# Decoding the output weights of a gated unit in three phases, and four moves of work in a fused attention, expert and gated-unit kernel

## The chip, the cores and the metric

The kernel runs on one core of a Trainium2 chip. The metric is the device time of one execution in microseconds. Five engines work side by side, each through its own queue in order: PE (TensorE, matrix products; its weight loads are shown apart as PEld), DVE (VectorE), ACT (ScalarE), POOL (GpSimd) and SP (SyncE, which issues most transfers).

## The reference

```
x   = attention(q, k, v, s)            # 4 x 8 heads, 576 rows of 64, causal, with a bias of cumulated s
e   = argmax(x @ w_gate); p = softmax's weight of e         # one expert of 8 for each of 2304 rows
x   = p * (relu(x @ w1[e]) @ w2[e])                         # 512 -> 1024 -> 512
xn  = x / sqrt(mean(x*x) + 1e-6) * rms_g
g   = xn @ moe2_w_gate;  val = xn @ moe2_w_val              # 512 -> 1536
out = (g * sigmoid(g) * val) @ moe2_w_out                   # 1536 -> 512
```
The three weights of the gated unit come as 64-bit floats. Products are made in single precision from a high and a low half of each operand, in three passes (high by high, high by low, low by high).

## The kernel before

**Stages.** Attention and routing come first, then the expert products (`moe`), then the gated unit (`glu`). PE, DVE and ACT run in the order in which the code issues (a manual schedule; for SP in `moe` too); POOL's order is set by the scheduler of the tile framework.

**Expert products.** `moe` runs eight slots. Slot 0 takes the first 256 rows of expert 0. For each of eight column blocks f, `gemm1` (L767) makes a hidden block; ACT writes its relu h in high halves (L770) and DVE the low halves (L771). `gemm2` (L783) makes four column blocks y from all eight f. Its first block needs the h of f = 0, 1, 2 ... one after another. Between the `gemm1` blocks of slot 0, `rank(n)` runs the next n steps of the last routing generator, small DVE instructions (L426 to L537) that place the rows and order the experts; the table `RANK` says how many steps before f = 0 and after each f.

After slot 0 come 128 more rows of expert 0 (`xl`, called the fill expert's rows here) in another form: their gate is applied by ACT (L722), `turn_tile` (L749 to L752) transposes them, `rows_gemm1` (L821, L823) makes the hidden rows `hr`, `turn_tile` transposes these into `hb`, with the low half by DVE (L752), and `rows_gemm2` (L832) multiplies. Its result is normed by `scaled_rows` (L839 to L842), called the yr chain here. The x of slot 1 is transposed beside it by `x_transpose` (L738 to L742). `finish` norms a slot's y: a product with ones (L805), a square root by ACT (L807), a reciprocal and four products by DVE (L808, L811); `keep` sends y to memory through SP. `split` makes high and low halves of the next expert weights (ACT L650, POOL L651).

**Gated unit.** `glu_head` is a generator that slot 7 of `moe` advances by one step after each f and each column block; it loads and decodes the first gated weights and splits the first rows `gx` (`glu_split_x`, L1038, L1039). `decode` turns two loads of 64-bit floats (`raw`) into single precision: on DVE two shifts of the low word (L1004), two joins with the high word (L1006); on ACT an absolute value (L1008); on DVE a maximum (L1010), a shift (L1012), an or (L1014) and the copy of the high half (L1016); on POOL the low half (L1017). There are four `raw` buffers.

The first product (L1061) goes over 12 blocks f, each for six groups g of 384 rows. The second product goes over `k.seq`, 72 steps: first f = 0 to 11 with g = 0 and 1 in turn (24 steps), then the other groups. A step (L1086) is nine matmuls, three passes for three tiles t of 128 rows. Its hidden block is split six steps ahead by ACT (L1076) and POOL (L1077) into a ring of twelve. Output weights 6 to 11 are decoded during the first 12 steps, two loads in each step with g = 1. After a group's last f ACT copies the three results (L1089) and POOL scatters them (L1090):

```
        if n < 24 and g == 1 and f + 6 < NF:
            decode(k, weights[0:2])
            weights = weights[2:]
            if f + 8 < NF:
                weights += load_out(k, f + 8)
        if n + ahead < len(k.seq):
            glu_split(k, n + ahead)
        glu_gemm2(k, acc, n)
```

Of the kernel before, what the change touches and what calls it, by code (L numbers as in the profile page):

```python
# [7 lines left out]
F32 = mybir.dt.float32  # L8
# [848 lines left out]
def moe(k, close):  # L857
# [40 lines left out]
    y = finish(k, 0, NA)  # L898
# [3 lines left out]
    turn_tile(k, k.hr[:, 512:1024], *[t[:, 4:8] for t in hb])  # L902
    split(k)
    x_transpose(k, 1, (2, 3), first)
    row = ids(k, k.x[1], first)
    keep(k, y, NA, 0)
    yr = y_tile(k, "yr")[:, 0:1024].rearrange("p (a n) -> p a n", a=2)
    k.yr = yr[:, 0, :]
    rows_gemm2(k, hb)
    keep_ids(k, row, column(k, 2))  # L910
# [44 lines left out]
RANK = (9, 0, 17, 10, 0, 0, 0, 0, 0)  # L955
# [43 lines left out]

def decode(k, loads):  # L1000
    nc = k.nc
    both = [(raw[:, :, 0], raw[:, :, 1], raw.bitcast(F32)[:, :, 1], w) for raw, w in loads]
    for low, high, hf, w in both:
        nc.vector.tensor_scalar(low, low, 29, None, op0=ALU.logical_shift_right)  # L1004
    for low, high, hf, w in both:
        nc.vector.scalar_tensor_tensor(low, high, 0xC0000000, low, op0=ALU.bitwise_and, op1=ALU.bitwise_or)  # L1006
    for low, high, hf, w in both:
        nc.scalar.activation(hf, hf, AF.Abs)  # L1008
    for low, high, hf, w in both:
        nc.vector.tensor_scalar(hf, hf, TINY, None, op0=ALU.max)  # L1010
    for low, high, hf, w in both:
        nc.vector.tensor_scalar(high, high, 3, 0x3FFFFFFF, op0=ALU.logical_shift_left, op1=ALU.bitwise_and)  # L1012
    for low, high, hf, w in both:
        nc.vector.tensor_tensor(high, high, low, op=ALU.bitwise_or)  # L1014
    for low, high, hf, w in both:
        nc.vector.tensor_copy(w[:, 0, :], hf)  # L1016
        nc.gpsimd.tensor_tensor(w[:, 1, :], hf, w[:, 0, :].bitcast(F32), op=ALU.subtract)  # L1017
# [62 lines left out]
def glu_gemm2(k, acc, n):  # L1080
    g, f = k.seq[n]
    w, c = k.wo[f], k.ring[n % 12]
    for t in range(3):
        cols = slice(128 * t, 128 * t + 128)
        for i, (a, b) in enumerate(((0, 0), (0, 1), (1, 0))):
            k.nc.tensor.matmul(acc[g][t], c[:, a, cols], w[:, b, :], start=f == 0 and i == 0, stop=f == 11 and i == 2)  # L1086
        if f == 11:
            o = new_raw(k).bitcast(F32).rearrange("p d two -> p (d two)")
            k.nc.scalar.copy(o, acc[g][t])  # L1089
            i = k.nc.gpsimd.indirect_dma_start(  # L1090
                out=k.out, out_offset=bass.IndirectOffsetOnAxis(ap=k.oid[:, g, t:t + 1], axis=0),
                in_=o, in_offset=None, bounds_check=NTOK - 1, oob_is_err=False,
            )
            of_rows(k, k.outs, i.ins, ())


def glu_head(k):
    glu_first(k)
    for g in range(3):
        glu_load(k, g)  # L1100
        if g == 0:
            weights = load_weights(k, 0)
    yield
    yield
    decode(k, weights[0:2])
    yield
    decode(k, weights[2:4])
    yield
    for n in (0, 0, 0, 0, 1, 2, 3, 4):
        if n:  # L1110
            glu_split_x(k, (n - 1) // 2, slice(2 * ((n - 1) % 2), 2 * ((n - 1) % 2) + 2))
        if n in (2, 4):
            glu_load(k, 2 + n // 2)
        yield


def glu(k):
# [66 lines left out]
    ahead = 6  # L1184
    for n, (g, f) in enumerate(k.seq):
        if f == 0:
            acc[g] = [k.psum.tile([128, 512], F32, name=f"go{k.uid()}", tag="b") for _ in range(3)]
        if n < 24 and g == 1 and f + 6 < NF:
            decode(k, weights[0:2])
            weights = weights[2:]  # L1190
            if f + 8 < NF:
                weights += load_out(k, f + 8)
        if n + ahead < len(k.seq):
            glu_split(k, n + ahead)
        glu_gemm2(k, acc, n)
# [185 lines left out]
```

## Time and profile before

| | |
|---|---|
| median of three runs | 929.44 us (929.34 to 929.82) |
| the profiled execution | 934.07 us, span 932.3 us |
| mean granted clock of TensorE | 0.988 of full speed |
| PE busy | 889.3 us, 95% of the span, 5684 matmuls |
| DVE, ACT, POOL busy | 460.2, 410.8, 332.9 us (49%, 44%, 36%) |
| attention and routing | to about 210 us of the span |
| expert products | about 210 to 460 us |
| first, second product of the gated unit | 460 to 761, 761 to 922 us |

Times in the profile are counted from the start of the span. A wait is an engine's idle time in front of an instruction, put down to what released it. Busy shares are averages over stages with different limits; what a stage is worth is read in the stage.

### The profile page before, as it was taken

Reading aid. Unit: us, or ns where it says so; the run is one execution under the profiler, and the core shown is the slowest. Engines: PE = TensorE matmul, PEld = TensorE weight load, DVE = VectorE, ACT = ScalarE, POOL = GpSimd, SP = SyncE. Lnnn points to the kernel's source line nnn. Section 1 sums busy time; section 2 is a strip of 40 time slices with the busy share of each in tenths; the row PEclk is TensorE's granted clock in tenths of the full one; section 3 lists DMA queues with packets and bytes.
Section 4 is the critical chain, followed back from the end, with each engine's and each line's share of the span. In section 5 each row is a group of like instructions: output and inputs, shape, how many; then the busy total and the mean of one; then the engine's idle time right before and its main releaser. Section 6 shows DMA issues by size and latency. Waiting matters only on the chain.

```text
span 932.3 us, 15830 instructions
## 1 busy us (share of the span) xinstructions
PE 889.3 (95%) x5684; PEld 781.1 (84%) x5684; DVE 460.2 (49%) x1339; ACT 410.8 (44%) x1009; POOL 332.9 (36%) x320
## 2 busy tenths in 40 slices
PE   6999999998799999999899999999999998899995
PEld 3666666668699999999899999999999995588884
DVE  4555664637524354544685555444554699700000
ACT  5887887873655566665531111111111122333310
POOL 2001321034566667676111110011100146797541
PEclk9999999999999999999999999999999999999998
DMA  7996686323646566666531101111011122110001
GB/s 236 291 295 193 180 233 183 97 97 90 227 154 194 174 193 195 196 182 210 166 102 46 46 26 43 46 46 45 27 43 46 46 100 81 47 68 35 35 34 37
DMA packets 51388, 111.59 MB, mean 120 GB/s; under 512 B 6064, under 2 KB 14027, under 8 KB 51299
## 3 DMA queue, kind: packets, MB, share of 16 engines
q1 hardware_dynamic: 48339, 100.95, 35.7%
q0 software_dynamic: 2912, 9.46, 2.7%
q8 instruction: 47, 0.77, 0.3%
q14 instruction: 42, 0.34, 0.1%
q10 hardware_dynamic: 48, 0.07, 0.0%
HBM read 89.69 MB, written 20.76 MB: 118 GB/s over the span
## 4 chain that ended last, share of the span: by engine, by line
PE 84%; DVE 6%; issue 4%; POOL 3%; ACT 2%; DMA 1%; POOLq 0%; DVEq 0%; ACTq 0%
PE gg L1061 32%; PE g L783 11%; PE g L767 8%; PE go L1086 8%; PE t L306 6%; PE pvy L352 5%; PE s L261 5%; PE tl L380 3%; PE sm L274 2%; DVE raw L1014 1%; DVE raw L1004 1%; PE xp L738 1%; PE r L832 1%; POOL gx5b L1077 1%; PE r L821 1%
## 5 line engine op out<-in xcount | busy, mean ns | idle before, releaser
L1061 PE MATMUL gg<-gx,ws 128*128 128x384 f32 x1728 | 300.4, 335 | 0.0
L1061 PEld LDWEIGHTS gg<-gx,ws 128*128 128x128 f32 x1728 | 299.6, 188 | 0.1
L651 POOL TENSOR_TENSOR u<-raw,u 128x1024 fp32r<-128x1024 f32 x64 | 154.3, 2422 | 104.4 <-ACT u L650 100.4
L1017 POOL TENSOR_TENSOR ws<-raw,ws 128x256 fp32r<-128x256 f32 x48 | 36.7, 786 | 259.2 <-DVE ws L1016 259.2
L783 PE MATMUL g<-h,u 128*128 128x256 f32 (+7 forms) x768 | 109.0, 301 | 5.4 <-DVE h L771 4.2
L783 PEld LDWEIGHTS g<-h,u 128*128 128x128 f32 x768 | 104.5, 194 | 6.5 <-DVE h L771 4.6
L767 PE MATMUL g<-xt,u 128*128 128x256 f32 (+7 forms) x768 | 104.2, 295 | 0.0
L1067 ACT ACTIVATE gh<-gg 128x384 f32<-128x384 f32 x72 | 35.3, 491 | 152.9 <-PE gg L1061 152.9
L767 PEld LDWEIGHTS g<-xt,u 128*128 128x128 f32 x768 | 101.4, 188 | 0.8
L1008 ACT ACTIVATE raw<-raw 128x256 f32<-128x256 f32 x72 | 28.1, 442 | 124.9 <-DVE raw L1006 112.4
L287 ACT ACTIVATE p<-sc,nm 128x128 f32<-128x128 f32 (+3 forms) x128 | 72.4, 572 | 12.0 <-DVE nm L247 8.3
L1068 DVE TENSOR_TENSOR gh<-gg,gh 128x384 f32<-128x384 f32 x72 | 40.0, 555 | 74.8 <-ACT gh L1067 74.8
L247 DVE CUSTOM_DVE_ANT_0 sc<-s,in 128x128 f32<-128x128 f32 (+3 forms) x128 | 57.5, 489 | 39.0 <-PE s L264 19.9
L650 ACT CAST u<-raw 128x1024 fp32r<-128x1024 f32 x64 | 67.2, 1050 | 4.0 <-DMA raw<-in_w 4.0
L339 ACT COPY pt<-t 128x512 f32<-128x512 f32 (+3 forms) x160 | 62.2, 433 | 11.6 <-PE t L306 7.4
L306 PE MATMUL t<-ident,p 128*128 128x128 f32 x400 | 62.2, 281 | 1.6 <-ACT p L287 1.5
L1069 DVE TENSOR_TENSOR gh<-gg,gh 128x384 f32<-128x384 f32 x72 | 40.2, 558 | 44.8 <-PE gg L1061 41.6
L791 DVE TENSOR_TENSOR sq<-sq,sn 128x256 f32<-128x256 f32 (+7 forms) x24 | 15.7, 653 | 87.8 <-ACT sn L790 87.8
L352 PE MATMUL pvy<-pt,vp 128*64 128x512 f32 (+4 forms) x320 | 50.8, 433 | 1.5 <-ACT pt L339 0.8
L261 PE MATMUL s<-in 64*128 64x128 f32 (+3 forms) x256 | 51.5, 491 | 0.0
L306 PEld LDWEIGHTS t<-ident,p 128*128 128x128 f32 x400 | 43.8, 141 | 6.9 <-ACT p L287 2.2
L234 POOL COPY in<-in 64x64 f32<-64x64 f32 x32 | 8.0, 251 | 116.0 <-DMA in<-in_q 106.0
(232 smaller groups left out, 1207.4 us busy)
## 6 DMA issues: line engine op xcount, KB each, us to landing
raw<-in_w SPq DMA_DIRECT2D x64, 512.0 KB, 4.3
in<-cumd SPq DMA_DIRECT2D x30, 256.0 KB, 5.1
xs<-zrow SPq DMA_DIRECT2D x8, 771.0 KB, 10.2
raw<-in_wg SPq DMA_DIRECT2D x24, 256.0 KB
raw<-in_wv SPq DMA_DIRECT2D x24, 256.0 KB, 3.0
raw<-in_wo SPq DMA_DIRECT2D x24, 256.0 KB, 2.6
vp<-in_v SPq DMA_DIRECT2D x16, 320.0 KB, 5.9
in<-in_q SPq DMA_DIRECT2D x16, 288.0 KB, 5.3
```

The source lines that it names most:

```text
L247: k.nc.vector.tensor_tensor_reduce(out=out, in0=ps, in1=bias, scale=-0.125, scalar=3e38, op0=ALU.add, op1=ALU.min, accum_out=accum)
L261: nc.tensor.matmul(ps[h], st.q[r, 128 * i:128 * i + 128], st.k[r, 0:w], start=True, stop=False)
L287: k.nc.scalar.activation(out, st.s[i, h][:, 0:w], AF.Exp, bias=st.nm[:, n:n + 1], scale=-1.0, accum_out=acc)
L306: nc.tensor.transpose(ps[:, off:off + 128], src[:, 128 * j:128 * j + 128], k.ident)
L339: nc.scalar.copy(b, a)
L352: nc.tensor.matmul(st.y[r, a - 64:512], st.v[:, h, j, :], k.pt[:, h, o:o + S - a], start=j == 0, stop=j == 4)
L650: nc.scalar.copy(w[:, :, 0, :], raw)
L651: nc.gpsimd.tensor_tensor(w[:, :, 1, :], raw, w[:, :, 0, :].bitcast(F32), op=ALU.subtract)
L767: nc.tensor.matmul(ps[:, 0:n], w[:, f % 4, a, 128 * kc:128 * kc + 128], x[b][:, kc, 0:n], start=kc == 0 and i == 0, stop=kc == 3 and i == 2)
L783: nc.tensor.matmul(ps[:, 0:n], w[:, f % 4, a, 128 * c:128 * c + 128], k.h[b][:, f, 0:n], start=f == 0 and i == 0, stop=f == 7 and i == 2)
L1061: nc.tensor.matmul(ps, w[:, m, a, 128 * kc:128 * kc + 128], b[:, kc, :], start=kc == 0 and n == 0, stop=kc == 3 and n == 2)
L1086: k.nc.tensor.matmul(acc[g][t], c[:, a, cols], w[:, b, :], start=f == 0 and i == 0, stop=f == 11 and i == 2)
```

## The change

It has five parts. (1) `finish` of slot 0 is issued after the transposes of `hb` and of slot 1's x instead of before them, its `keep` after `rows_gemm2`, and `yr` uses the buffer of `hr`. (2) `RANK` spreads the last ten steps of the ranking over the blocks after f = 2 to f = 7. (3) `glu_head` decodes in three phases, low, high and split, in successive steps, and its splits of `gx` come one step later. (4) In the second product the two loads of an output weight are decoded over three steps: low at g = 0, high at g = 1, split at the next g = 0, where ACT makes the copy of the high half; the split of the hidden block is issued ahead of them. (5) The last four steps of the last group go tile by tile instead of block by block, and the last result is copied in two halves by ACT and DVE.

```
@@ moe
-    y = finish(k, 0, NA)
     hb = [...]
     turn_tile(k, k.hr[:, 0:512], *[t[:, 0:4] for t in hb])
     x_transpose(k, 1, (0, 1), first)
     turn_tile(k, k.hr[:, 512:1024], *[t[:, 4:8] for t in hb])
+    x_transpose(k, 1, (2, 3), first)
     split(k)
-    x_transpose(k, 1, (2, 3), first)
+    y = finish(k, 0, NA)
     row = ids(k, k.x[1], first)
-    keep(k, y, NA, 0)
-    yr = y_tile(k, "yr")[:, 0:1024].rearrange("p (a n) -> p a n", a=2)
+    yr = k.hr.rearrange("p (a n) -> p a n", a=2)
     k.yr = yr[:, 0, :]
     rows_gemm2(k, hb)
+    keep(k, y, NA, 0)
@@
-RANK = (9, 0, 17, 10, 0, 0, 0, 0, 0)
+RANK = (9, 0, 17, 3, 1, 1, 1, 2, 2)
@@ decode, cut into decode_low (L1004, L1006), decode_high (L1008 to L1014) and
+def decode_split(k, loads, cast):
+    nc = k.nc
+    for low, high, hf, w in parts(loads):
+        cast(w[:, 0, :], hf)
+        nc.gpsimd.tensor_tensor(w[:, 1, :], hf, w[:, 0, :].bitcast(F32), op=ALU.subtract)
...
@@ glu_head
-    decode(k, weights[0:2])
+    decode_low(k, weights[0:2])
     yield
-    decode(k, weights[2:4])
+    decode_high(k, weights[0:2])
+    decode_low(k, weights[2:4])
     yield
-    for n in (0, 0, 0, 0, 1, 2, 3, 4):
+    decode_split(k, weights[0:2], k.nc.vector.tensor_copy)
+    decode_high(k, weights[2:4])
+    yield
+    decode_split(k, weights[2:4], k.nc.vector.tensor_copy)
+    yield
+    for n in (0, 0, 0, 1, 2, 3, 4):
...
@@ second product
-        if n < 24 and g == 1 and f + 6 < NF:
-            decode(k, weights[0:2])
-            weights = weights[2:]
-            if f + 8 < NF:
-                weights += load_out(k, f + 8)
         if n + ahead < len(k.seq):
             glu_split(k, n + ahead)
+        if half:
+            decode_split(k, half, k.nc.scalar.copy)
+            half = None
+        if n < 24 and f + 6 < NF:
+            if g == 0:
+                decode_low(k, weights[0:2])
+            else:
+                decode_high(k, weights[0:2])
+                half, weights = weights[0:2], weights[2:]
+                if f + 8 < NF:
+                    weights += load_out(k, f + 8)
         glu_gemm2(k, acc, n)
@@ glu_gemm2 (glu_part is the body of the loop over t)
+    if n < len(k.seq) - LASTF:
+        for t in range(3):
+            glu_part(k, acc, n, t)
+    elif n == len(k.seq) - 1:
+        for t in range(3):
+            for m in range(LASTF):
+                glu_part(k, acc, n + 1 - LASTF + m, t)
@@ glu_part, at f == 11 (LASTF = 4)
+        if g == NG - 1 and t == 2:
+            k.nc.scalar.copy(o[:, 0:256], acc[g][t][:, 0:256])
+            k.nc.vector.tensor_copy(o[:, 256:512], acc[g][t][:, 256:512])
+        else:
             k.nc.scalar.copy(o, acc[g][t])
```

How the instructions move is shown at three places; the numbers in names are buffers. First DVE in the fill expert's rows: `hb` and `xt` are the low halves of the transposed rows (L752, L742), L808 and L811 are `finish`.

```order
 L791 TENSOR_TENSOR sq_3057<-sq_3057,sn_3_3199 128x256
+L752 TENSOR_TENSOR hb_3241<-xq_3242,hb_3240 128x4x128
+L742 TENSOR_TENSOR xt_3250<-xp_0_3251,xt_3249 128x312
+L742 TENSOR_TENSOR xt_3250<-xp_1_3252,xt_3249 128x312
+L752 TENSOR_TENSOR hb_3241<-xq_3263,hb_3240 128x4x128
+L742 TENSOR_TENSOR xt_3250<-xp_2_3270,xt_3249 128x312
+L742 TENSOR_TENSOR xt_3250<-xp_3_3271,xt_3249 128x312
 L808 RECIPROCAL sq_3057<-sq_3057 128x256
 L811 SCALAR_TENSOR_TENSOR y_3056<-y_3056,gv,sq_3057 128x256 x4
-L752 TENSOR_TENSOR hb_3249<-xq_3250,hb_3248 128x4x128
-L742 TENSOR_TENSOR xt_3258<-xp_0_3259,xt_3257 128x312
-L742 TENSOR_TENSOR xt_3258<-xp_1_3260,xt_3257 128x312
```
All six low halves now stand ahead of `finish`.

Second DVE in slot 0, the low halves h of f = 3 and f = 4 (g_3, g_4) and the ranking (nb, oover and oends are its results).

```order
 L516 CAST nb<-ogot 1x7
+L771 SCALAR_TENSOR_TENSOR h_2839<-g_3_2946,h_2838 128x256
 L518 TENSOR_SCALAR oover<-ocnt 1x1
...
 L527 TENSOR_TENSOR nb<-oflag 1x1
+L771 SCALAR_TENSOR_TENSOR h_2839<-g_4_2987,h_2838 128x256
 L529 CAST nb<-oover 1x8
...
 L537 CAST nb<-oends 1x8
-L771 SCALAR_TENSOR_TENSOR h_2839<-g_3_2965,h_2838 128x256
-L771 SCALAR_TENSOR_TENSOR h_2839<-g_4_2996,h_2838 128x256
 L771 SCALAR_TENSOR_TENSOR h_2839<-g_5_3011,h_2838 128x256
```
The first two move up between the ranking's steps; those of f = 5 to 7 stay behind them.

Third ACT in the second product, before and then with the change. CAST from gh is the high half of a hidden block for the ring (L1076, now L1093), ACTIVATE the absolute value (L1008, now L1015), CAST from raw the copy of a weight's high half (L1027).

```order
L1076 CAST gx5b_12139<-gh454_9445 128x384
L1008 ACTIVATE raw660_12088<-raw660_12088 128x256
L1008 ACTIVATE raw661_12090<-raw661_12090 128x256
L1076 CAST gx5b_12139<-gh455_9446 128x384
L1076 CAST gx5b_12139<-gh454_9445 128x384
L1008 ACTIVATE raw664_12141<-raw664_12141 128x256
```

```order
L1093 CAST gx5b_12139<-gh455_9446 128x384
L1015 ACTIVATE raw660_12088<-raw660_12088 128x256
L1015 ACTIVATE raw661_12090<-raw661_12090 128x256
L1093 CAST gx5b_12139<-gh454_9445 128x384
L1027 CAST gx2b_11983<-raw660_12088 128x256
L1027 CAST gx2b_11983<-raw661_12090 128x256
L1093 CAST gx5b_12139<-gh455_9446 128x384
L1015 ACTIVATE raw664_12141<-raw664_12141 128x256
```
The copies of a pair of loads now stand on ACT, one hidden block behind their absolute values; POOL's order of L1077 and L1017 does not change.

## Rows read from the trace of the kernel before

**Rows 1.** Waits of PE, whole span: who waits, for whom, total us, times, longest us
```profile
PE r L832 <- DVE hb L752: 5.0, 1, 5.0
PE g L783 <- DVE h L771: 4.2, 2, 2.7
```

**Rows 2.** Timeline, slot 0's gemm2: start us, us, engine, line, operation, count, [idle before]
```profile
223.82 1.35 PE L783 MATMUL g<-h,u 128*128 128x256 f32 x10
...
227.84 6.27 PE L783 MATMUL g<-h,u 128*128 128x256 f32 x38 [2.67 <-DVE h L771]
...
232.42 0.72 ACT L722 ACTIVATE xl<-xl 128x512 f32<-128x512 f32 x1 [0.56 <-DMA xl<-xs]
...
233.95 0.60 PE L749 MATMUL xq<-ident,xl 128*128 128x128 f32 x4
```

**Rows 3.** Windows: stretch; busy us (count) of PE, PEld, DVE, ACT, POOL; clock; DMA share
```profile
230.00:231.00 1.00, 1.00 (x7) 1.00 (x7) 0.00 (x0) 0.00 (x0) 0.00 (x0) 0.50 0.10 25
...
784.00:790.00 6.00, 4.67 (x18) 3.22 (x18) 5.74 (x13) 1.57 (x4) 3.62 (x5) 1.00 0.26 89
```

**Rows 4.** Timeline, the fill expert's rows
```profile
249.11 0.50 PE L832 MATMUL r<-u,hb 128*128 128x512 f32 x1
...
250.13 3.82 DVE L811 SCALAR_TENSOR_TENSOR y<-y,gv,sq 128x256 f32<-128x256 f32 x4
...
253.87 0.68 DVE L752 TENSOR_TENSOR hb<-xq,hb 128x512 fp32r<-128x512 f32 x1
...
254.60 7.42 PE L832 MATMUL r<-u,hb 128*128 128x512 f32 x23 [4.99 <-DVE hb L752]
...
261.63 1.86 PEld L767 LDWEIGHTS g<-xt,u 128*128 128x128 f32 x12
```

**Rows 5.** Timeline, slot 7
```profile
438.96 1.72 DVE L811 SCALAR_TENSOR_TENSOR y<-y,gv,sq 128x268 f32<-128x268 f32 x4
...
448.96 11.74 PE L783 MATMUL g<-h,u 128*128 128x248 f32 x86 [1.50 <-DVE h L771]
```

**Rows 6.** Timeline, weight loads of the second product, groups 0/1 and group 2
```profile
760.79 5.39 PEld L1086 LDWEIGHTS go<-ws0b,gx1b 128*128 128x128 f32 x24
...
822.80 4.07 PEld L1086 LDWEIGHTS go<-ws0b,gx1b 128*128 128x128 f32 x18
...
826.91 4.04 PEld L1086 LDWEIGHTS go<-gx0b,gx1b 128*128 128x128 f32 x18
```

**Rows 7.** Timeline, one period of the second product
```profile
783.03 1.12 POOL L1077 TENSOR_TENSOR gx5b<-gh,gx5b 128x384 fp32r<-128x384 f32 x1 [1.81 <-ACT gx5b L1076]
...
783.21 2.38 DVE L1014 TENSOR_TENSOR raw<-raw 128x256 uint32<-128x256 uint32 x2
...
785.52 0.49 DVE L1016 CAST gx2b<-raw 128x256 fp32r<-128x256 f32 x2
...
785.88 1.50 POOL L1017 TENSOR_TENSOR gx2b<-raw,gx2b 128x256 fp32r<-128x256 f32 x2 [0.57 <-DVE gx2b L1016]
785.92 1.61 DVE L1004 TENSOR_SCALAR raw<-raw 128x256 uint32<-128x256 uint32 x2
...
792.08 1.62 DVE L1004 TENSOR_SCALAR raw<-raw 128x256 uint32<-128x256 uint32 x2
```

**Rows 8.** Timeline, the same instructions with the other engine idle
```profile
480.46 0.49 DVE L1004 TENSOR_SCALAR raw<-raw 128x256 uint32<-128x256 uint32 x2
...
482.79 0.76 DVE L1014 TENSOR_TENSOR raw<-raw 128x256 uint32<-128x256 uint32 x2
...
812.80 1.99 POOL L1077 TENSOR_TENSOR gx5b<-gh,gx5b 128x384 fp32r<-128x384 f32 x2
```

**Rows 9.** Page, part 5: shapes, count | busy us, mean ns | idle before, releaser
```profile
L1008 ACT ACTIVATE raw<-raw 128x256 f32<-128x256 f32 x72 | 28.1, 442 | 124.9 <-DVE raw L1006 112.4
```

**Rows 10.** Timeline, end of the program
```profile
921.29 1.29 ACT L1089 COPY raw<-go 128x512 f32<-128x512 f32 x2 [0.16 <-PE go L1086]
...
923.99 0.98 POOL L1090 DMA_INDIRECT out<-raw,oid  x1 [0.30 <-issue]
```

More of the change, by code (lines that the diff above doesn't have):

```diff
@@ L997, in as_f32, with parts, decode_low, decode_high @@
     nc.vector.tensor_tensor(high, high, low, op=ALU.bitwise_or)
-def decode(k, loads):
[L1001 to L1017, printed above, removed]
+def parts(loads):
+    return [(raw[:, :, 0], raw[:, :, 1], raw.bitcast(F32)[:, :, 1], w) for raw, w in loads]
+def decode_low(k, loads):
+    nc = k.nc
+    for low, high, hf, w in parts(loads):
+        nc.vector.tensor_scalar(low, low, 29, None, op0=ALU.logical_shift_right)
+    for low, high, hf, w in parts(loads):
+        nc.vector.scalar_tensor_tensor(low, high, 0xC0000000, low, op0=ALU.bitwise_and, op1=ALU.bitwise_or)
+def decode_high(k, loads):
+    nc = k.nc
+    for low, high, hf, w in parts(loads):
+        nc.scalar.activation(hf, hf, AF.Abs)
+    for low, high, hf, w in parts(loads):
+        nc.vector.tensor_scalar(hf, hf, TINY, None, op0=ALU.max)
+    for low, high, hf, w in parts(loads):
+        nc.vector.tensor_scalar(high, high, 3, 0x3FFFFFFF, op0=ALU.logical_shift_left, op1=ALU.bitwise_and)
+    for low, high, hf, w in parts(loads):
+        nc.vector.tensor_tensor(high, high, low, op=ALU.bitwise_or)
+def decode_split(k, loads, cast):
+    nc = k.nc
+    for low, high, hf, w in parts(loads):
+        cast(w[:, 0, :], hf)
+        nc.gpsimd.tensor_tensor(w[:, 1, :], hf, w[:, 0, :].bitcast(F32), op=ALU.subtract)
+def decode(k, loads):
+    decode_low(k, loads)
+    decode_high(k, loads)
+    decode_split(k, loads, k.nc.vector.tensor_copy)
 HALVES = (slice(0, 256), slice(256, 512))
@@ L1077, in glu_split, with glu_part, glu_gemm2 @@
     nc.gpsimd.tensor_tensor(c[:, 1, :], h, c[:, 0, :].bitcast(F32), op=ALU.subtract)
-def glu_gemm2(k, acc, n):
+def glu_part(k, acc, n, t):
     g, f = k.seq[n]
     w, c = k.wo[f], k.ring[n % 12]
[L1083 to L1088, printed above, removed]
-            k.nc.scalar.copy(o, acc[g][t])
[L1090 to L1094, printed above, removed]
+    cols = slice(128 * t, 128 * t + 128)
+    for i, (a, b) in enumerate(((0, 0), (0, 1), (1, 0))):
+        k.nc.tensor.matmul(acc[g][t], c[:, a, cols], w[:, b, :], start=f == 0 and i == 0, stop=f == 11 and i == 2)
+    if f == 11:
+        o = new_raw(k).bitcast(F32).rearrange("p d two -> p (d two)")
+        if g == NG - 1 and t == 2:
+            k.nc.scalar.copy(o[:, 0:256], acc[g][t][:, 0:256])
+            k.nc.vector.tensor_copy(o[:, 256:512], acc[g][t][:, 256:512])
+        else:
+            k.nc.scalar.copy(o, acc[g][t])
+        i = k.nc.gpsimd.indirect_dma_start(
+            out=k.out, out_offset=bass.IndirectOffsetOnAxis(ap=k.oid[:, g, t:t + 1], axis=0),
+            in_=o, in_offset=None, bounds_check=NTOK - 1, oob_is_err=False,
+        )
+        of_rows(k, k.outs, i.ins, ())
+LASTF = 4
+def glu_gemm2(k, acc, n):
+    if n < len(k.seq) - LASTF:
[5 more added lines that the diff above has]
+                glu_part(k, acc, n + 1 - LASTF + m, t)
 def glu_head(k):
@@ L1183, in glu @@
     acc = {}
-    ahead = 6
+    ahead, half = 6, None
     for n, (g, f) in enumerate(k.seq):
```

## Prediction

> **What bounds the kernel now.** TensorE (PE) is busy for most of the span, so every microsecond to win is one in which it stands still or runs at the lower of its two clock levels. I read the list of PE's waits first, then the timeline around each, then the second product of the gated unit, where the waits are short but come again and again.
>
> The list of waits [rows 1] names two sources of some size: the row product of the fill expert (L832) waits 5.0 us once for the low half of hb, and the expert's second product (L783) waits twice for the low half of h, 4.2 us in all. The timeline gives their places. In slot 0 [rows 2] PE has issued ten matmuls when it runs into h of f = 3, which stands on DVE behind the last steps of the ranking. [...] The wait for hb [rows 4]: L752 starts at 253.87, after four L811 of 3.82 us; PE resumes at 254.60 after 4.99 us. The third wait lies in slot 7 [rows 5], behind the decoding of the first gated weights.
>
> In the second product a step is nine matmuls; 18 of them take 826.91 - 822.80 = 4.11 us, so a step takes 2.06 us at full speed [rows 6]. The first 24 steps run from 760.79 to 822.80, 62.0 us where 24 x 2.06 = 49.4 would do: 12.6 us are lost. The pattern repeats with the decoding of two loads: 792.08 - 785.92 = 6.16 us for two steps, which PE could do in 4.11 [rows 7]. Six such periods are touched by the change. DVE is busy 5.74 of 6 us and POOL 3.62 of 6 there, with the clock at 1.00 [rows 3]. But DVE is mostly blocked: its pair of L1014 takes 2.38 us beside POOL's L1077, its pair of L1004 takes 1.61 beside L1017 [rows 7]; alone they take 0.76 and 0.49 [rows 8]. POOL loses little by it (1.12 a piece against 1.99 / 2 = 1.00 alone). So a period is about POOL's busy time plus the DVE time during which POOL has nothing to do.
>
> **The change, part by part.**
>
> *finish behind the transposes.* The 24 matmuls of L832 have a step's shape, 0.228 us each. The last 23 ran from 254.60 to 261.63, when the next weight load starts [rows 4]: 7.03 us against 23 x 0.228 = 5.24. So the place costs 4.99 of idling and 1.8 of slow matmuls, 6.8 us. In the new order L752 and L742 wait for nothing but ACT's casts, which no longer have the square root and its table load ahead of them. The first half of hb is then ready while PE still does transposes, the second while PE does the first twelve matmuls. finish moves beside the 5.5 us of L832. There it has reciprocal and L811 ahead of L841 on DVE, for which the yr chain waits; L811 takes 1.72 alone [rows 5] or 3.82 beside POOL [rows 4]. POOL's next split is issued by ACT behind that chain, so I take the short one: gain 6.8. If it is the long one, 2.1 comes back: 4.7. Upper end 7.1, if the transposes close up as well.
>
> *RANK.* The same instructions stand before the last L771 of slot 0 but for the final two steps, so h of f = 7 comes no earlier; only the matmuls before it do. What is late next is the transpose of xl: its gate L722 waits for a DMA, starts at 232.42 and ends at 233.14, while PE came there at 233.95 [rows 2]. The scatter behind that DMA is not moved. So at most 0.8, at least 0; I take 0.7, since the slow matmuls leave that much room.
>
> *Head in three phases.* DVE does the same work before the last h of slot 7; f = 3 comes earlier, f = 4 then lies behind the second high phase. PE waits a little later for about as long. Upper end the 1.5 us of [rows 5] and the slow matmuls behind it, 2.2; lower end one pair of copies, now between two L771, -0.5 (0.49 [rows 7]). It is nearer the lower end: 0.4. The splits of gx come one step later; the last two column blocks of the expert product cover them. If they did not, PE would wait for a gx at the start of the gated unit.
>
> *Second product in three phases.* The two copies L1016 leave DVE; ACT makes them instead. On DVE they took 0.49 us, and POOL stood 0.57 idle until L1017 could start [rows 7]. An ACT pass of this size takes 0.44 [rows 9]; ACT is busy 1.57 of 6 us [rows 3], so two more do not make it the bound. The 0.57 fall out of a period, and splitting the phases lets POOL do some work while DVE waits for ACT's abs: I take 0.65, and 6 x 0.65 = 3.9. Lower end nothing, since POOL keeps its order and L1017 now waits behind ACT's queue; upper end PE's own pace, 6 x (6.16 - 4.11) = 12.3. The estimate lies near the lower end, because ten of DVE's twelve instructions of a period do not change and POOL's 3.6 us stay.
>
> [...]
>
> *End.* Now the three results of the last group are ready together; the second and third ACT copies start at 921.29 and, by 0.59 for one, near 921.99, and POOL issues the last scatter at 923.99 [rows 10]. With the order turned, the first two scatters go out 24 and 12 matmuls earlier (5.5 and 2.7 us). Only the third is left, copied in halves by ACT and DVE. A half takes between 0.3 (half of 0.59) and 0.6, so with a little for the issue it goes out between 922.4 and 922.8. Gain 1.2 to 1.6, taken 1.4.
>
> *Nothing.* keep behind L832: SP's queue has the same order. yr in hr's buffer: it spares a wait for that keep which the move would else bring; its writer comes after hr's last reader. The matmuls are as many as before.
>
> **Sum:** 6.8 + 0.7 + 0.4 + 3.9 + 1.4 = 13.2. Against the profiled execution, 934.07 (span 932.3), this gives 920.9. The median of the runs is 929.44, 0.5% below that execution; all stalls taken lie in the program and not in what surrounds it, so I take the same 13.2 off: 916.2.
>
> **Rivals.**
> 1. *The second product reaches PE's pace or nearly.* If DVE's tensor_scalar instructions other than L1004 do not wait for POOL, the phases overlap and a period falls to some 4.6: 6 x 1.56 = 9.4 in place of 3.9, 910.7. For it: no row shows L1010 or L1012 blocked. Against: L1004 is the same kind and is blocked.
> 2. *The second product gains nothing*, since ACT's queue now holds copies that wait for DVE ahead of the next split of the hidden layer, and L1077 follows it: 920.1. For it: L1077 starts each time from an ACT release [rows 7]. Against: two copies less on the busiest engine.
> 3. *A new wait in the fill expert's rows*: finish is late, L841 with it, PE idles again and drops its clock: about half of the 6.8 lost, 919.6.
> [...]
> 5. *Slower.* The clock falls in the second product. It stayed at 1.00 there, with PE busy 4.67 of 6 us [rows 3]; it fell where PE idled for 2.67 and more in one piece. [...] Against: the twelve-deep ring spreads what is ready over several steps.
> That the change does not do what it says is excluded for the orders, which are shown above.
>
> **How the numbers follow.** Chances: forecast 0.61, rival 1 0.10, rival 2 0.12, rival 3 0.09, rival 4 0.05, rival 5 0.02, unnamed 0.01. The forecast's own range is 914.0 to 918.5, from the ends of its terms. The range 912.5 to 920.5 takes in rivals 2 and 3 and leaves out 1, 4 and 5. No change means within 0.2% (1.9 us), about what a measurement of this kernel can tell: all cases but rival 5 lie well below 927.5. Faster 0.96, same 0.02, slower 0.02.
>
> **What would show it.** In the profile after: no wait of L832 for hb above 0.5 us, and L832's 24 matmuls in 5.5 us at clock 1.00; the transpose of xl directly behind its gate; a wait for h in slot 7 still there, for a later f; periods of the second product near 5.5 us with L1016's successor on ACT; the last scatter issued within 1 us of PE's last matmul. Wrong would be a period at 4.1 or above 6, a wait in L832, or a clock below 1.00 between 760 and 910.

## The result, and the profile after

The changed kernel takes **916.04 us** (median of four runs, 915.48 to 917.04), the kernel before 929.62 beside it: ratio 0.9855, 95% interval 0.9838 to 0.9872. The forecast was 916.2. The profiled execution took 916.49 us, its span 914.8, at a mean granted clock of 0.995. PE is busy for 97% of the span.

A total can come out right from wrong terms, so both traces are cut at the same instructions: the first matmul of a stage, the first weight load of the second product and of its group 2, the issue of the last scatter, the end of the span. "Again" is a second profile of each kernel, taken together with the experiments below. Times are in us.

| stretch | before | before again | changed | changed again | gain | forecast |
|---|---|---|---|---|---|---|
| attention and routing | 211.86 | 212.20 | 208.72 | 211.36 | none | none |
| slot 0, first product | 11.96 | 12.00 | 11.95 | 11.95 | none | none |
| slot 0, second product, to L821 | 16.32 | 16.28 | 15.94 | 16.04 | 0.3 | 0.7 |
| fill expert's rows, to slot 1 | 21.72 | 21.90 | 14.75 | 14.75 | 7.1 | 6.8 |
| slots 1 to 7, to slot 7's second product | 182.77 | 182.77 | 182.75 | 182.74 | none | none |
| slot 7, second product, to the gated unit | 15.90 | 15.86 | 13.44 | 13.41 | 2.5 | 0.4 |
| first product of the gated unit | 300.26 | 300.26 | 300.25 | 300.24 | none | none |
| second product, first 24 steps | 62.01 | 62.00 | 57.66 | 57.66 | 4.3 | 3.9 |
| the rest, to the last scatter's issue | 101.19 | 101.19 | 100.41 | 100.41 | 0.8 | 1.4 |
| from there to the end of the span | 8.31 | 8.34 | 8.93 | 8.64 | -0.5 | none |

Attention took 208.72 and 211.36 us in two executions of the same changed kernel, so such a difference is no part of the change; what sets it was not shown. Ratios are taken only between runs on one chip. Some 3 us of it would be most of the 4.6 us by which the profiled execution of before lay above its median.

**The waits of PE.** L832's wait for hb is gone. What is left:

```profile
PE g L783 <- DVE h L771: 3.4, 4, 1.0
...
PE go L1102 <- POOL gx1b L1094: 1.8, 2, 0.9
...
PE go L1102 <- POOL gx5b L1094: 1.4, 2, 0.9
PE go L1102 <- POOL gx4b L1094: 1.4, 2, 0.9
```
The waits for h (4.2 us in two pieces in [rows 1]) are now four short ones, in slots 0 and 7. In the second product PE is now released, but for one wait, by POOL's low half of a hidden block (L1094).

**Fill expert's rows**, the timeline of the changed kernel that answers to [rows 4]:

```profile
244.89 0.68 DVE L752 TENSOR_TENSOR hb<-xq,hb 128x512 fp32r<-128x512 f32 x1
...
245.69 5.84 PE L832 MATMUL r<-u,hb 128*128 128x512 f32 x24
...
250.04 1.67 DVE L811 SCALAR_TENSOR_TENSOR y<-y,gv,sq 128x256 f32<-128x256 f32 x4
251.13 1.85 PEld L767 LDWEIGHTS g<-xt,u 128*128 128x128 f32 x12
...
252.67 0.16 DVE L841 RECIPROCAL ss<-ss 128x1 f32<-128x1 f32 x1 [0.96 <-ACT ss L840]
```
The second half of hb is ready at 245.57, before PE begins L832, and the 24 matmuls pass in 5.4 us to the next weight load at 251.13. L811 takes the short time (1.67) and is done at 251.71, before L841 is due.

**Slot 0 and its clock**, timeline and one window (as in [rows 2, 3]):

```profile
223.67 0.62 PE L783 MATMUL g<-h,u 128*128 128x256 f32 x3 [0.95 <-DVE h L771]
...
224.89 5.57 PE L783 MATMUL g<-h,u 128*128 128x256 f32 x32 [0.61 <-DVE h L771]
...
229.59 0.72 ACT L722 ACTIVATE xl<-xl 128x512 f32<-128x512 f32 x1 [2.46 <-DMA xl<-xs]
230.37 0.65 PE L749 MATMUL xq<-ident,xl 128*128 128x128 f32 x4
```

```profile
226.00:227.00 1.00, 1.00 (x7) 1.00 (x6) 0.00 (x0) 0.53 (x2) 0.00 (x0) 0.50 0.07 16
```
The one wait of 2.67 us became two of 0.95 and 0.61, but the clock fell all the same. PE reaches the transpose of xl 0.06 us behind its gate. In the second profile the clock stayed at 1.00 here, the same 32 matmuls took 4.04 us, and PE then waited 1.51 us for xl: the stretch is as long, as its end is set by xl's transfer.

**Slot 7**, as in [rows 5]:

```profile
434.11 1.65 PE L783 MATMUL g<-h,u 128*128 128x248 f32 x13
436.77 0.62 PE L783 MATMUL g<-h,u 128*128 128x248 f32 x3 [1.01 <-DVE h L771]
438.26 9.45 PE L783 MATMUL g<-h,u 128*128 128x248 f32 x80 [0.87 <-DVE h L771]
```
PE waits 1.88 us where it waited 1.26 + 1.50, and the clock stays at 1.00 behind it (from 436 to 450). The 1.26 is a wait for ACT's high half of h, which the forecast did not count; in the kernel before it stands just ahead of the 1.50 of [rows 5]:

```profile
447.08 0.38 PE L783 MATMUL g<-h,u 128*128 128x248 f32 x1 [1.26 <-ACT h L770]
```

**A period of the second product**, timeline of DVE, ACT and POOL (as in [rows 7]):

```profile
771.03 0.75 DVE L1021 TENSOR_TENSOR raw<-raw 128x256 uint32<-128x256 uint32 x2
771.48 0.77 ACT L1027 CAST gx2b<-raw 128x256 fp32r<-128x256 f32 x2 [1.89 <-DVE raw L1021]
771.70 0.48 DVE L1007 TENSOR_SCALAR raw<-raw 128x256 uint32<-128x256 uint32 x2
771.99 1.71 POOL L1028 TENSOR_TENSOR gx2b<-raw,gx2b 128x256 fp32r<-128x256 f32 x2 [1.24 <-ACT gx2b L1027]
772.11 1.87 DVE L1009 SCALAR_TENSOR_TENSOR raw<-raw 128x256 uint32<-128x256 uint32 x2
...
773.66 1.18 POOL L1094 TENSOR_TENSOR ws1b<-gh,ws1b 128x384 fp32r<-128x384 f32 x1
773.90 1.29 DVE L1017 TENSOR_SCALAR raw<-raw 128x256 f32<-128x256 f32 x2
...
775.03 1.03 POOL L1094 TENSOR_TENSOR gx1b<-gh,gx1b 128x384 fp32r<-128x384 f32 x1 [0.19 <-POOL ws1b L1094]
775.11 1.30 DVE L1019 TENSOR_SCALAR raw<-raw 128x256 uint32<-128x256 uint32 x2
...
777.01 0.48 DVE L1007 TENSOR_SCALAR raw<-raw 128x256 uint32<-128x256 uint32 x2
```
A period is 777.01 - 771.70 = 5.31 us in place of 6.16. Six weights are decoded, five such periods apart: the first takes 5.8 us and the others 5.3 (before, all five 6.2). Together that is 3.8 of the 4.35 us of the stage. The blocked instructions have changed: the join L1021 (before, L1014, 2.38) and the shift L1007 (before, L1004, 1.61) run at their pace alone (0.75 and 0.48), as POOL waits for ACT's copy meanwhile; now the join L1009, the maximum L1017 and the shift L1019 are long beside POOL. POOL's own idle time has changed places too: it stands 1.24 us ahead of L1028 (0.57 before), but hardly any ahead of the hidden blocks' low halves (0.19, before 1.81).

**The end**, as in [rows 10]:

```profile
903.76 0.86 PE L1102 MATMUL go<-gx4b,ws1b 128*128 128x512 f32 x3
904.71 0.37 ACT L1106 COPY raw<-go 128x256 f32<-128x256 f32 x1 [2.20 <-PE go L1102]
905.16 0.42 DVE L1107 COPY raw<-go 128x256 f32<-128x256 f32 x1 [112.19 <-ACT raw L1106]
905.87 0.97 POOL L1110 DMA_INDIRECT out<-raw,oid  x1 [2.11 <-DVE raw L1107]
```
The two halves run one behind the other: DVE's copy starts after ACT's has ended (905.08), and its row puts the wait down to that copy. The last scatter is issued 1.25 us behind the end of PE's last matmul (904.62), where the forecast had at most 1 us.

### The profile page after: what moved, and what is told of

It reads as the page before. It is cut to its first block, busy times and chain, and to the rows that moved or that the text cites. A ratio compares the mean times of both kernels' runs of the same rounds, so it can differ in the third digit from the quotient of the medians.

```text
span 914.8 us, 15811 instructions
## 1 busy us (share of the span) xinstructions
PE 884.5 (97%) x5684; PEld 779.1 (85%) x5684; DVE 454.3 (50%) x1328; ACT 416.6 (46%) x1021; POOL 333.7 (36%) x320
## 4 chain that ended last, share of the span: by engine, by line
PE 90%; DVE 6%; ACT 1%; POOL 1%; issue 1%; DMA 0%; POOLq 0%; DVEq 0%; ACTq 0%
PE gg L1078 33%; PE go L1102 13%; PE g L783 11%; PE g L767 9%; PE t L306 6%; PE s L261 5%; PE pvy L352 5%; PE tl L380 3%; PE sm L274 2%; DVE raw L1009 1%; PE xp L738 1%; DVE raw L1019 1%; DVE raw L1017 1%; PE r L832 1%; PE s L264 1%
## 5 line engine op out<-in xcount | busy, mean ns | idle before, releaser
L1028 POOL TENSOR_TENSOR ws<-raw,ws 128x256 fp32r<-128x256 f32 x48 | 38.1, 814 | 255.3 <-DVE ws L1027 255.3
L1015 ACT ACTIVATE raw<-raw 128x256 f32<-128x256 f32 x72 | 28.6, 440 | 104.7 <-DVE raw L1009 94.1
```

## The experiments

Ten edited kernels, and both kernels once more as they are. In the tables "slot 0", "fill", "slot 7", "24 steps" and "to scatter" are the stretches of the table above; the ratio is to the kernel before on the same chip, with its 95% interval. The times expected start from the result's 929.6 and 916.0 us, but on the chips of the experiments the kernel before takes 932.7 to 933.3; so compare ratios and stretches, not the times as such.

**1. The kernel before, again.**

> The kernel before once more, unedited. In its first profile the expert products begin 3.1 us later than in the changed kernel's (first product of slot 0 at 211.86 against 208.72), though the change touches nothing ahead of them. If that belonged to the one profiled execution, this profile has them near 208.7 and a span near 928. If it belongs to the kernel, they stand near 211.9 again and the span near 932. Rows to be seen again either way: L832 waiting about 5.0 us, two waits of L783 for h of 4.2 us in all, periods of the second product of 6.16 us.

933.51 us, ratio 0.9997 (0.9987 to 1.0007); attention 212.20 us, span 932.8. So the 3 us are not that one execution's. Nor are they the kernel's: the changed kernel takes 211.36 in run 6, and the profiles of all runs here lie between 210.7 and 212.2. What made 208.72 of it in the changed kernel's first profile, the runs don't show. Every other stretch repeats within 0.2 us.

**2. The first part alone**, the kernel before with

```
-    y = finish(k, 0, NA)
     hb = [...]
...
     split(k)
+    y = finish(k, 0, NA)
...
     rows_gemm2(k, hb)
+    keep(k, y, NA, 0)
```

> The kernel before with the first part alone (finish behind the transposes, keep behind the row product, yr in the buffer of hr). Forecast's theory: the 5.0 us wait of L832 and the slow matmuls behind it go, 6.8 us, so some 922.8. Rival (finish late, a new wait in the yr chain or in slot 1): 3.4 us, 926.2. If the pieces of the change only pay together: under 2 us, above 927.6.

927.00 us, ratio 0.9932 (0.9917 to 0.9947), 6.3 us less by the medians; in the trace the stretch is 14.76 in place of 21.90, 7.1 less. Of the other stretches only attention (0.6 less) and the time behind the last scatter's issue (8.0 in place of 8.3) move by over 0.1 us. The term of 6.8 stands, by itself.

**3. The head as before**, the changed kernel with

```
-    decode_low(k, weights[0:2])
-    yield
-    decode_high(k, weights[0:2])
-    decode_low(k, weights[2:4])
...
+    decode(k, weights[0:2])
+    yield
+    decode(k, weights[2:4])
```

> The changed kernel with the head decoded in two steps as before (third part undone). Forecast's term: 0.4 us slower, 916.4, with PE's wait in slot 7 about as long as with three phases. What the trace of the changed kernel suggests instead: the stretch from slot 7's second product to the gated unit goes back from 13.4 to about 15.9 us, the clock falls to 0.50 again there, 918.5.

921.83 us, ratio 0.9876 (0.9861 to 0.9892), where the changed kernel has 0.9851: some 2.3 us slower. The two intervals overlap at their ends (the ratio of run 6 reaches 0.9867), so the stretch decides: slot 7 takes 15.92 us again, in place of 13.4. The term of 0.4 was too small.

**4. The copies of the high halves back on DVE**, phases kept:

```
-            decode_split(k, half, k.nc.scalar.copy)
+            decode_split(k, half, k.nc.vector.tensor_copy)
```

> The changed kernel with the copies of the weights' high halves in the second product on DVE again, the three phases kept. If the copies on ACT carry most of the second product's gain (the forecast's 0.57 of 0.65 a period), the period goes from 5.31 to about 5.9 and the time to 919.5 or so. If the phases carry it, the period stays near 5.4 and the time near 916.5. If DVE and POOL have to take turns for all of their work, the copies add 0.49 a period: 919.0.

922.54 us, ratio 0.9892 (0.9875 to 0.9908). Beside 929.6 that would be 919.6, as expected if the copies carry most. The 24 steps take 60.81 us: the phases, with the hidden block's split ahead of them, bring 1.2 of the 4.35. The period is 6.16 us (from one L1007 to the next, 776.93 and 783.10), as in the kernel before: without the copies on ACT the phases shorten no period. In this profile the granted clock is at 0.50 for 3.4 us from 794.5 on (16 weight loads from 793.73 take 5.09 us, where the same 16 took 3.50 a period before), so 60.81 may hold some of that.

**5. The copies on ACT, without the phases:**

```
+        if n < 24 and g == 1 and f + 6 < NF:
+            decode_low(k, weights[0:2])
+            decode_high(k, weights[0:2])
+            decode_split(k, weights[0:2], k.nc.scalar.copy)
...
         if n + ahead < len(k.seq):
             glu_split(k, n + ahead)
```

> The changed kernel with each output weight decoded whole at g = 1 and ahead of nothing else, as before, but with ACT making the copy of the high half: the copies without the phases. With the copies back on DVE and the phases kept, the way from the start of the second product to the last scatter took 161.2 us where the changed kernel takes 158.1 and the kernel before 163.2. If copies and phases add up, this one takes about 160.0, 2 us over the changed kernel. If the copies do all the work and the phases nothing, 158.2. If the copies on ACT need the phases (ACT's queue holding them behind a decoding that is still running), 162 or more.

921.60 us, ratio 0.9884 (0.9869 to 0.9899). The 24 steps take 60.42 us, and the way to the last scatter 160.8, nearest to the 160.0 expected if copies and phases add up. The last four periods take 5.28 to 5.45 us, so the copies shorten them without the phases. What is lost is one step; the timeline of ACT and PE and a window show why:

```profile
766.19 0.76 ACT L1027 CAST gx2b<-raw 128x256 fp32r<-128x256 f32 x2 [1.10 <-DVE raw L1021]
...
767.42 0.73 PE L1102 MATMUL go<-gx0b,gx5b 128*128 128x512 f32 x2 [1.68 <-ACT gx5b L1093]
769.58 8.82 PE L1102 MATMUL go<-gx0b,gx5b 128*128 128x512 f32 x25 [1.43 <-POOL gx5b L1094]
```

```profile
771.00:773.00 2.00, 2.00 (x6) 1.59 (x5) 1.84 (x7) 1.54 (x5) 1.02 (x1) 0.50 0.01 4
```
With the decoding in one piece and ahead of the hidden block's split, ACT's copies wait for DVE, and the split stands behind them in ACT's queue: this is rival 2's mechanism. PE waits 1.68 and 1.43 us for one step, the granted clock falls to 0.50, and the 25 matmuls that follow take 8.82 us instead of 25 x 0.228 = 5.7: this is rival 5's. Without the slow matmuls the 24 steps would have taken some 57.3, an estimate; by it the copies on ACT do nearly all the work, and the rest of part 4 keeps PE's waits in small pieces. Whether that is owed to the phases or to the split's place ahead of them was not tried: this run undoes both.

**6. The changed kernel, again.**

> [...] Ratio to before 0.985 again. Stages as in its first profile: slot 0's second product 15.9 us, fill expert's rows 14.75, slot 7's second product 13.4, second product of the gated unit to the last scatter 158.1.

918.71 us, ratio 0.9851 (0.9836 to 0.9867), and the stages of the table above. The three below ran beside it.

**7. An output weight over three steps:**

```
+        j, phase = divmod(n, 3)
+        if j + 6 < NF:
+            if phase == 0:
+                decode_low(k, weights[0:2])
+            elif phase == 1:
+                decode_high(k, weights[0:2])
+            else:
+                decode_split(k, weights[0:2], k.nc.scalar.copy)
```

> The changed kernel with an output weight decoded over three steps of the second product instead of two (low, high and split each in a step of its own, six weights in 18 steps). A period then holds three steps of PE, 6.17 us, and 3 x 1.0 + 1.5 us of POOL and 3.1 of DVE. [...] If DVE and POOL take turns strictly, a period takes 7.6 and 18 steps lose 8.6 us: no gain, 916 to 917. If the lost time was owed to the ring's depth and not to the decoding, no gain either.

915.66 us, ratio 0.9818 (0.9805 to 0.9831), 3 us better than the changed kernel. The 24 steps take 54.90 us: 2.8 won of the 8.3 over PE's own 49.4. The period is 6.13 to 6.15 us for three steps, which is PE's own pace and not the 7.6 of strict turns, and from the eleventh step to the twentieth PE does not wait. What is left lies at both ends: PE waits in the fifth and tenth steps, and in the last four for the weights themselves (0.7 us twice for POOL's L1028), which come late now. DVE has no time to spare: from 776 to 782 it is busy all 6.00 us.

**8. The last result in one copy:**

```
-        if g == NG - 1 and t == 2:
-            k.nc.scalar.copy(o[:, 0:256], acc[g][t][:, 0:256])
-            k.nc.vector.tensor_copy(o[:, 256:512], acc[g][t][:, 256:512])
-        else:
-            k.nc.scalar.copy(o, acc[g][t])
+        k.nc.scalar.copy(o, acc[g][t])
```

> The changed kernel with the last result copied whole by ACT instead of in two halves by ACT and DVE. In the changed kernel the two halves ran one after the other (0.37, then 0.42 us), the last scatter 0.87 + 0.3 us behind the last product. If they can't run together, one copy of 0.59 is 0.25 us better, and the time 915.8. The forecast's theory, halves side by side, would make it 0.2 us worse.

919.32 us, ratio 0.9852 (0.9838 to 0.9865): no difference by the runs. In the trace the last scatter is issued 0.3 us sooner (100.11 us behind the 24 steps, with halves 100.41). The halves cost what was to be expected of two copies in a row. This run's profile also has the clock at 0.50 in slot 7 (14.91 us, 13.41 in run 6), with the changed head.

**9. Three moves at PE's remaining waits for h:** the head with one phase a step, xl's transposes one column block later, and for slot 0's last two splits

```
-            nc.gpsimd.tensor_tensor(w[:, :, 1, :], raw, w[:, :, 0, :].bitcast(F32), op=ALU.subtract)
+            for a in range(2):
+                for c in (slice(0, 256), slice(256, 512)):
+                    nc.gpsimd.tensor_tensor(w[:, a, 1, c], raw[:, a, c], w[:, a, 0, c].bitcast(F32), op=ALU.subtract)
```

> The changed kernel with three moves at its remaining waits of PE for h: the head's decoding in five steps instead of four (one phase a step), POOL's last two splits of slot 0's weights in eight pieces of a quarter each, and xl's transposes one column block later. Theory: in slot 0 two small DVE instructions of the ranking (1.87 and 2.08 us where their neighbours take 0.2) waited each for the end of a 2.4 us POOL instruction; in pieces of 0.7 they wait under 0.7, the ranking ends some 2.5 us earlier, PE's idling in slot 0 falls from 2.0 to under 0.5 and its clock stays up: 2 to 3 us of the 15.9. In slot 7 the 1.9 us of waiting go for the most part. Sum 3.5 to 4.5: 912. [...]

923.80 us, ratio 0.9908 (0.9893 to 0.9924): 5 us slower than the changed kernel. Its trace says which of the three did it. Timeline of DVE and POOL in slot 0's first product, the changed kernel and then this one:

```profile
212.99 4.75 POOL L651 TENSOR_TENSOR u<-raw,u 128x1024 fp32r<-128x1024 f32 x2 [5.88 <-ACT u L650]
...
213.56 1.87 DVE L449 TENSOR_TENSOR ob<-oh,base 128x40 f32<-128x40 bf16 x1
...
215.47 0.20 DVE L451 TENSOR_REDUCE bt<-ob 128x5 f32<-128x40 f32 x1
...
215.58 0.19 DVE L453 TENSOR_REDUCE se<-ex 128x5 f32<-128x40 f32 x1
...
215.68 2.08 DVE L455 TENSOR_SCALAR xt<-tid 128x5 f32<-128x5 f32 x1
```

```profile
215.50 4.91 POOL L654 TENSOR_TENSOR u<-raw,u 128x256 fp32r<-128x256 f32 x7 [5.88 <-ACT u L650]
...
216.08 0.22 DVE L449 TENSOR_TENSOR ob<-oh,base 128x40 f32<-128x40 bf16 x1
...
216.54 0.42 DVE L455 TENSOR_SCALAR xt<-tid 128x5 f32<-128x5 f32 x1
...
219.77 0.70 DVE L499 TENSOR_TENSOR ogt<-okey 1x49 f32<-1x49 f32 x1
```
So L449 and L455 had been held up by POOL's two instructions, of 2.39 us each, and beside pieces they take 0.22 and 0.42. Not every small instruction was held: L451 and L453 took 0.20 and 0.19 inside POOL's second one. But POOL is then at it for longer, later steps such as L499 wait 0.6 to 0.7 each, and the ranking ends 1.1 us earlier, not 2.5. The loss comes from the second move: ACT's split of the next weights, which waits for a transfer, stood ahead of the cast of xb. Timeline of ACT and PE:

```profile
237.28 1.04 ACT L650 CAST u<-raw 128x1024 fp32r<-128x1024 f32 x1 [3.17 <-DMA raw<-in_w]
...
238.77 0.59 ACT L756 CAST xb<-xq 128x512 fp32r<-128x512 f32 x1
...
239.41 0.50 PE L826 MATMUL r<-u,xb 128*128 128x512 f32 x1 [2.20 <-ACT xb L756]
241.71 7.16 PE L826 MATMUL r<-u,xb 128*128 128x512 f32 x23 [1.79 <-DVE xb L757]
```
Behind the two waits the 23 matmuls take 7.16 us in place of 23 x 0.228 = 5.2 (the 23 of [rows 4], with the clock at 0.50 from 252 to 258, take 7.42). Number 12 has the same move with the cast ahead of the split, and loses 0.8 us there in place of 3.7. In slot 7 PE waited 1.79 us in one piece in place of 1.88 in two: one phase a step changed nothing, as DVE only comes to the decoding after the norm of the slot before.

**10. All low halves on DVE**, over three steps:

```
+            glu_split(k, n + ahead, k.nc.vector if n < 18 else None)
...
+                decode_split(k, weights[0:2], k.nc.scalar.copy, k.nc.vector)
```

> The changed kernel with an output weight decoded over three steps, and with the low halves of weights and hidden blocks made by DVE instead of POOL while the decoding lasts, so that POOL has nothing to do there. Three steps then hold 3 x 0.55 + 0.76 + 3.1 = 5.5 us of DVE work in place of 3.1 of DVE and 4.5 of POOL. Theory (a DVE instruction between SBUF tiles waits for the end of POOL's, so the two engines' times nearly add up and set the pace): DVE's pairs take 0.49, 0.63 and 0.76 throughout, PE waits only in the first ten steps for what is left over from the first product, and the first 24 steps take 51 to 52.5 us against 57.7 (54.9 with POOL, spread over three steps): 3 us better than that. Rival: DVE itself is the bound, whatever POOL does (its own chain through ACT's absolute value and casts); then 55 us or more.

912.19 us, ratio 0.9782 (0.9768 to 0.9795). The 24 steps take 50.82 us, 1.4 over PE's own 49.4; what is left is the two waits in the fifth step. Timeline of DVE and one window:

```profile
769.78 0.55 DVE L1094 TENSOR_TENSOR ws1b<-gh,ws1b 128x384 fp32r<-128x384 f32 x1
770.25 0.49 DVE L1017 TENSOR_SCALAR raw<-raw 128x256 f32<-128x256 f32 x2
770.65 0.49 DVE L1019 TENSOR_SCALAR raw<-raw 128x256 uint32<-128x256 uint32 x2
771.05 0.75 DVE L1021 TENSOR_TENSOR raw<-raw 128x256 uint32<-128x256 uint32 x2
```

```profile
770.00:776.00 6.00, 6.00 (x28) 4.93 (x27) 6.00 (x21) 3.55 (x10) 0.00 (x0) 1.00 0.41 140
```
Every pair takes what it takes alone (0.48 to 0.49, the joins 0.75), one weight with three hidden blocks takes 4.64 us (from one L1007 to the next, 768.70 and 773.34), where number 7 took 6.13, and PE does not stop. One engine, doing all of the work, is faster here than two.

**11. The same, with a later head,** the splits of hidden blocks 4 and 5 ahead of the last decoding, and one last copy:

```
+    for n in (1, 2, 3, 4):
+        if n == 2:
+            decode_low(k, weights[2:4])
+        if n == 3:
+            decode_high(k, weights[2:4])
+        if n == 4:
+            decode_split(k, weights[2:4], k.nc.vector.tensor_copy)
```

> The kernel with all low halves on DVE, and three moves more: the head decodes its second pair of loads behind the column blocks of slot 7's second product instead of before them, the hidden blocks 4 and 5 are split ahead of the last decoding of the first product, and the last result is copied whole. Theory: DVE is late in slot 7 because the norm of the slot before (1.83 + 1.72 us) stands ahead of the decoding; with half of the decoding moved behind, PE no longer waits for h there: 13.4 to 11.6 us. The two splits cost PE 1.8 us of waiting around the fifth step, which goes. Together 3.5 to 4 us better than with all low halves on DVE alone. Rival: the gated unit then waits for its own first weights, which come later by two column blocks; then the first product loses what slot 7 gains.

907.86 us, ratio 0.9732 (0.9718 to 0.9745). Slot 7 takes 11.02 us, and its second product is one unbroken row:

```profile
437.17 11.18 PE L783 MATMUL g<-h,u 128*128 128x248 f32 x96
```
The first product does not pay for it (300.26), and the 24 steps take 49.56. One row shows the blocking from the other side, 12 us into the second product, where POOL still splits a weight while DVE runs without a pause (busy 3.80 of 3.80 us):

```profile
760.42 3.70 POOL L1028 TENSOR_TENSOR gx2b<-raw,gx2b 128x256 fp32r<-128x256 f32 x2 [3.03 <-DVE gx2b L1027]
```
Such a pair takes 1.50 us in [rows 7], where DVE is the one that waits.

**12. Slot 0 as well:** number 11 with xl's transposes behind the third column block, this time ahead of the splits, and the pieces of number 9.

> The kernel with all low halves on DVE and the later head, and now slot 0: xl's transposes one column block later, with their casts ahead of the next split on ACT this time, and POOL's two splits of 2.4 us in eight pieces of 0.7. With xl in its old place a clock that stays up brings nothing, PE then waits 1.5 to 1.6 us for xl's transfer. Theory: that wait goes behind the third column block (2.95 us of matmuls) and the ranking ends 1.1 us earlier, so the stretch from slot 0's second product to the row product goes from 16.1 to between 13.9 and 14.5 us, and the time from 907.9 to about 906. Rival: the later transposes make the row product wait for their low half, as in the run with the three moves at PE's waits for h, where a split stood ahead of the cast; then 16 us or more and no gain.

907.66 us, ratio 0.9722 (0.9709 to 0.9735), against 0.9732 not to be told apart. The stretch fell from 16.12 to 13.86, as expected, but 0.8 us came back behind it (the fill expert's rows 15.58 in place of 14.75), and the rest is within what attention varies. The best version is number 11 or 12, some 11 us below the changed kernel.

| kernel | slot 0 | fill | slot 7 | 24 steps | to scatter |
|---|---|---|---|---|---|
| before again | 16.28 | 21.90 | 15.86 | 62.00 | 101.19 |
| 2 first part alone | 16.25 | 14.76 | 15.89 | 61.96 | 101.18 |
| 3 head as before | 15.70 | 14.76 | 15.92 | 57.61 | 100.41 |
| 4 copies on DVE | 15.84 | 14.76 | 13.46 | 60.81 | 100.41 |
| 5 copies only | 15.59 | 14.76 | 13.43 | 60.42 | 100.41 |
| changed again | 16.04 | 14.75 | 13.41 | 57.66 | 100.41 |
| 7 three steps | 15.63 | 14.75 | 15.02 | 54.90 | 100.41 |
| 8 one copy | 15.85 | 14.75 | 14.91 | 57.65 | 100.11 |
| 9 three moves | 16.18 | 18.46 | 13.46 | 57.66 | 100.41 |
| 10 all on DVE | 15.89 | 14.76 | 13.43 | 50.82 | 100.35 |
| 11 and later head | 16.12 | 14.75 | 11.02 | 49.56 | 100.10 |
| 12 and slot 0 | 13.86 | 15.58 | 11.02 | 49.56 | 100.10 |

## Why the prediction was right, and where not

The time was right, and the two large terms with it; three small terms were mis-sized. The head was taken 2.1 us too low, the end some 1 us too high, and the ranking 0.3 to 0.5 us too high. That these nearly cancel is luck. The forecast's own range, 914.0 to 918.5, does not follow from the ends of its terms as it says: these add up to gains of 5.4 and 24.0 us.

- *finish* (6.8 forecast, 7.0 to 7.1 measured): each step held. Both halves of hb are ready before PE comes, the 24 matmuls run at a clock of 1.00 (245 to 251), L811 takes its short time. Run 2 shows that the part needs none of the others.
- *RANK* (0.7; 0.24 to 0.4 in the two profiles of the changed kernel, 0.2 to 0.7 in all nine with the new table and xl in its old place; no run has this part alone): the cap was named rightly, xl's transfer. The reason given, "the slow matmuls leave that much room" (the 38 of [rows 2], with the clock at 0.50 in [rows 3]), missed that the clock might fall again. Where it fell, PE met the gate as the forecast said; where it did not, PE waited 0.7 to 1.6 us for xl. Both end alike.
- *Head* (0.4; 2.5): the step that failed is "PE waits a little later for about as long", with the choice near the lower end. PE waits 1.88 in place of 2.76, and the slow matmuls behind the wait, some 1.6 us, go where the clock stays up. The upper end, 2.2, was below what came, as it left 0.7 us for the slow matmuls. The clock's part is not sure of coming (the row behind this list). Of the seven profiles with the changed head (the changed kernel twice, runs 4, 5, 7, 8 and 10) two have the clock's fall, runs 7 and 8 (slot 7 takes 15.02 and 14.91 us, 13.41 to 13.46 in the other five); the four with the old head all do (15.86 to 15.92).
- *Second product* (3.9; 4.35, period 5.51 forecast and 5.31 measured): the size held, and the reason in part. The copies on ACT carry the period (6.16 with them on DVE in run 4, 5.28 to 5.45 with them on ACT and no phases in run 5), and are worth 3.2 where the phases are there (60.81 against 57.66), near the 3.4 counted for them. But "The 0.57 fall out of a period" is not what happened: POOL's wait for the copy grew to 1.24 us, and its wait ahead of the hidden blocks shrank from 1.81 to 0.19. What held is the sum behind it: a period is about POOL's busy time (now 1.71 + 1.18 + 1.03) plus the DVE time in which POOL has nothing to do (1.24 + 0.19). Number 10 shows the general cause: with POOL out of the way, DVE does a weight and three hidden blocks in 4.64 us, where DVE and POOL together took 6.13.
- *End* (1.4; 0.8 to the last scatter, at most 0.5 in the span): "copied in halves by ACT and DVE" was taken to run side by side. They run in a row, 0.37 and 0.42. The order by tiles alone, with one copy, brings 1.1 (run 8). And the 8.0 to 8.3 us from the last scatter's issue to the end of the span became 8.6 to 9.0 in every kernel with the new end, which the forecast did not count; why was not tried.

The row of slot 7 in run 7's timeline, after the same two waits as in the changed kernel's:

```profile
440.59 11.03 PE L783 MATMUL g<-h,u 128*128 128x248 f32 x80 [0.88 <-DVE h L771]
```
The 80 matmuls that took 9.45 us take 11.03 here.

Of the rivals: 1 fails on its own condition, since L1017 and L1019, which it took to be free, are blocked (1.29 and 1.30 the pair, 0.63 and 0.49 alone). 2's mechanism shows in a row, but it did not cost the gain: ACT's copies do wait for DVE (1.89 us ahead of L1027), with the split of the next hidden block behind them in ACT's queue. In run 5, where that split stands behind a whole decoding, PE waits for it. 3 shows no row. 4 is that DVE and POOL take strict turns for all of their work. A period would then need 2 x 1.00 + 1.50 us of POOL and 3.09 of DVE, from L1004 to the end of L1014 ([rows 7, 8]), 6.6 in all; it takes 5.31, so the times do not add up in full. What the traces show is single pairs of instructions that hold each other up, in both directions: L455 took 2.08 us behind POOL's instruction and 0.42 beside pieces, POOL's pair 3.70 behind DVE and 1.50 without. L451 and L453 were not held (0.20 and 0.19), so the theory of run 10 does not stand for every DVE instruction. Which instructions are held, and how much of the two engines' work overlaps, no run was made to show. 5 did not happen in the changed kernel's two traces. It did in run 5, and the clock fell in the second product for 3.4 us in run 4 and even in the control (from 791.8 on; 11 weight loads from 792.80 take 3.62 us, 2.46 in run 6 from 773.78), where the 24 steps took 62.00 all the same. That "it fell where PE idled for 2.67 and more in one piece" was read from too few rows: in slot 7 of the kernel before it fell behind waits of 1.26 and 1.50, to 0.50 for 3.4 us (450 to 453 and a part of the microsecond on either side).

For the whole change, where 13.2 was forecast, the traces give 14.4 and 14.8 us (17.5 and 15.6 between the spans, less 3.1 and 0.8 of attention), the medians 13.6 and 14.3. With slot 7's 1.5 us coming in some executions only, that is as near as it can be read.

## What to carry to other kernels

Where two engines block each other, look at the pairs of rows that are long beside each other and short alone, and ask whether one engine could do all of it: here work moved off POOL to a busy DVE was worth 4.1 us more than spreading the same work over time. When a wait is shortened, cost the clock behind it apart from the wait, and as a chance, not as a certainty. Two copies of one tile on two engines are not parallel until a row shows it.

## What the runs showed of the hardware that was not expected

- A DVE instruction over 128 x 5 elements took 2.08 us beside a POOL instruction of 2.4 us, and 0.42 with POOL's work cut in four pieces.
- After waits of the same length and place, the granted clock fell in some executions and not in others (80 matmuls in 9.45 or 11.03 us).
- Attention took 208.7 us in one profile and 210.7 to 212.2 in all others, for every kernel; what sets it was not tried.
